# The first two batches of a fused attention and SwiGLU kernel: query copies, scores, the table load and the dummy products in another order

## The chip, the cores and the metric

The kernel runs on one core of a Trainium2 chip. The metric is the device time of one execution in microseconds. Six executions of the kernel before took 236.55 to 238.45 us, median 237.5.

## What is computed

For each of 8 batches and 8 heads, 576 positions of width 64 attend to 32 memory slots; then a SwiGLU block runs over 4608 rows. From the reference:

```
a = softmax(phi)                       # over the 32 slots of each position
k_m = einsum('bhsm,bhsd->bhmd', a, k)  # and v_m from v
attn = softmax(q @ k_m.T / sqrt(64))   # b h s 32
x = (attn @ v_m), rows (b, s), columns (h, d): 4608 x 512
g = x @ w_gate                         # 512 x 1536
out = (silu(g) * (x @ w_val)) @ w_out
```

## The kernel before, in words

Engines: TensorE (PE) multiplies, with PEld its weight loads; VectorE is DVE, ScalarE is ACT, GpSimd is POOL, and SyncE (SP) issues transfers. Each engine takes its instructions in the order in which the program writes them; the whole order is written by hand (`tc.manual_schedule()`), and engines wait for one another through semaphores only.

The work goes by batch. For batches 0 and 1, which are prepared together at the start, each batch passes these steps:

- `phi_exp_masked` (L181): ACT takes exp(phi) into a tile with zeros in the other half of each head pair.
- `k_items` (L337) gives two items. `denominators` multiplies by ones (L244) and takes the reciprocal on DVE (L262, L346). `sums` multiplies keys by exp(phi) in 36 small products (`direct`, L313, products at L319) and copies the result to SBUF in four pieces (L333).
- `q_items` (L822) gives three items, each a call of `q_T` (L371): six transposes of the queries on PE (L377), then one copy of 128x768 from PSUM into `t_qT` by the engine that a letter names, "v" for DVE (L333) or "a" for ACT (L331).
- `scores(b, g)` (L386), for the two head groups g: eight products (L390), then two exponentials on ACT (L401).
- `z_inv(b, g)` (L412): two products with a block matrix of ones (L417), a logarithm of each on ACT (L420), and one exponential of the negative (L422), which is the inverse of the softmax sum.
- `norm(b, g)` (L444): DVE multiplies scores and inverse sums (L446).
- `v_direct` (L361): the same 36 products for the values, and four copies (L333).
- `u_half` (L829) multiplies the values with a half chunk of the gate weights (which = 0) or of the val weights (1), products at L466; the two results leave PSUM by the engines of its letters (ACT L488, DVE L492).
- `gv_gate` (L518) multiplies that with the normed scores (L509), and ACT takes Silu (L526). The val product and the multiplication on DVE (L532) are put in a list and run later by `flush_mul`.

After that the two batches run slot by slot through the weights' three chunks, then the output products (L720) of a batch run beside the next batch.

PSUM is handed out as eight banks in a ring: `bank` takes the first free one, `done` puts it at the end. `warm(n)` (L859) is dummy work: products of the ones matrix with itself, n times 128 columns, at most 512 in one, into a bank that goes back to the head of the ring.

ACT keeps one set of function tables; `preload_act_table_set` (L854, L941) changes it, from exponential and logarithm to Silu and back once for each batch.

The loads of the start come from POOL's queue in the order keys 0, queries 0, keys 1, queries 1, values 0, values 1, then the gate and val weights by halves of the first chunk, then the other chunks (L877 to L908). From the ninth on, POOL waits ahead of an issue for an earlier transfer to land.

The order of the start is this hand-written list (L912 to L951), of which the change touches all but the first lines:

```
    warm(104)
    k0, k1 = k_items(0, "vvvv"), k_items(1, "vvvv")
    q0, q1 = q_items(0, "vvv"), q_items(1, "vvv")
    run(k0)
    warm(8)
    run(k1[:1])
    warm(4)
    run(q0)
```

Of the kernel before, what the change touches and what calls it, by code (L numbers as in the profile page):

```python
# [14 lines left out]
def kernel(  # L15
# [19 lines left out]
    nc = tc.nc  # L35
# [39 lines left out]
    def bank(shape, dtype, name):  # L75
        tag = free.pop(0)
        t = ps.tile(shape, dtype, tag=tag, name=name)
        held[id(t)] = tag, t
        return t

    def done(*tiles):

        for t in tiles:
            free.append(held.pop(id(t))[0])
# [34 lines left out]
    def q_of(b, i, g, r):  # L119

        h = NG * i + g
        return qTs[b][64 * r:64 * r + 64, :, NC * h:NC * h + NC]
# [190 lines left out]
    def direct(b, which):  # L313

        p = bank([128, NP // 2, NG, M], FP32, "p_mT")
        for n in range(NP // 2):
            for j in range(JK):
                for o in range(2):
                    nc.tensor.matmul(  # L319
                        p[64 * o:64 * o + 64, n],  # L320
                        lhsT=kvs[b][:, which, 2 * n + o, j * D:(j + 1) * D],
                        rhs=masked[b][:, j, :, 2 * n + o],
                        start=(j == 0),
                        stop=(j == JK - 1),
                        tile_position=(0, 64 * o),
                    )
        return p

    def copy(eng, out, in_):
        if eng == "a":  # L330
            nc.scalar.copy(out=out, in_=in_)  # L331
        else:
            nc.vector.tensor_copy(out=out, in_=in_)  # L333
# [27 lines left out]
    def v_direct(b, engs):  # L361

        p = direct(b, 1)
        dst = kTs[b][:, 2].rearrange("p (n o m) -> p n o m", n=NP // 2, o=2)
        for x, e in enumerate(engs):
            g, o = x % 2, x // 2
            copy(e, dst[64 * g:64 * g + 64, :, o], p[64 * o:64 * o + 64, :, g])
        done(p)
        scaled.add(b)

    def q_T(b, n, eng="v"):  # L371

        k = NS // 3
        pq = bank([128, k, 128], BF16, "p_q")
        for x in range(k):
            y = k * n + x
            nc.tensor.transpose(pq[:, x], qs[b][:, 128 * y:128 * y + 128], ident)  # L377
        if n == 0:
            qTs[b] = att.tile([128, NS, 128], BF16, tag="qT", name="t_qT")
        copy(eng, qTs[b][:, k * n:k * n + k], pq)  # L380
        done(pq)

    def gv_banks():
        return [bank([128, CH], FP32, f"p_{'gv'[r]}") for r in range(2)]

    def scores(b, g):  # L386
        p = gv_banks()
        for i in range(NP):
            for r in range(2):
                nc.tensor.matmul(  # L390
                    p[r][32 * i:32 * i + 32, 0:HALF],
                    lhsT=kTs[b][64 * r:64 * r + 64, g, 32 * i:32 * i + 32],
                    rhs=q_of(b, i, g, r),
                    start=True,
                    stop=True,
                    tile_position=(64 * r, 32 * i),
                )
        e = att.tile([128, 2, HALF], BF16, tag=f"E{g}", name="t_E")
        for r in range(2):
            scale = rks[b][:, g:g + 1] if b in rks else sm_scale  # L400
            nc.scalar.activation(  # L401
                out=e[:, r].rearrange("p (c s) -> p c s", c=NC),
                in_=p[r][:, 0:HALF].rearrange("p (s c) -> p c s", c=NC),
                func=AF.Exp,
                scale=scale,
            )
        done(*p)
        es[b, g] = e
# [3 lines left out]
    def z_inv(b, g):  # L412

        p = gv_banks()
        lz = att.tile([128, 2, HALF], FP32, tag="lz", bufs=3, name="t_lz")
        for r in range(2):
            nc.tensor.matmul(  # L417
                p[r][:, 0:HALF], lhsT=bones, rhs=es[b, g][:, r], start=True, stop=True
            )
            nc.scalar.activation(out=lz[:, r], in_=p[r][:, 0:HALF], func=AF.Ln)  # L420
        done(*p)
        nc.scalar.activation(out=lz, in_=lz, func=AF.Exp, scale=-1.0)  # L422
        lzs[b, g] = lz
# [20 lines left out]
    def norm(b, g):  # L444
        a = att.tile([128, 2, HALF], BF16, tag=f"A{g}", name="t_A")
        nc.vector.tensor_tensor(out=a, in0=es.pop((b, g)), in1=lzs.pop((b, g)), op=ALU.mult)  # L446
        atts[b, g] = a
# [6 lines left out]
    def u_round(b, parts, evac):  # L454


        banks = []
        for which, c, halves in parts:
            w0, w1, h0, h1 = which[0], which[-1] + 1, halves[0], halves[-1] + 1
            n = (h1 - h0) * HC  # L460
            p = [bank([128, CH], FP32, f"p_u{g}") for g in range(NG)]
            for w in which:
                o = (w - w0) * n
                for i in range(NP):
                    for g in range(NG):
                        nc.tensor.matmul(  # L466
                            p[g][32 * i:32 * i + 32, o:o + n],
                            lhsT=kTs[b][64 * g:64 * g + 64, 2, 32 * i:32 * i + 32],
                            rhs=w_part(w, c, i, g, halves),
                            start=True,  # L470
                            stop=True,
                            tile_position=(64 * g, 32 * i),
                        )
            for g in range(NG):
                if (b, c, g) not in Us:
                    u_buffer(b, c, f"U{c}")
                if len(which) == 1:
                    dst = Us[b, c, g][:, h0:h1, w0]
                else:
                    dst = Us[b, c, g][:, h0]  # L480
                src = p[g][:, 0:(w1 - w0) * n].rearrange("p (a f) -> p a f", f=HC)
                banks.append((dst, src, p[g], rSs[b][:, g:g + 1] if b in scaled else None))
        for (t, p, home, r), e in zip(banks, evac):
            if e == "a":
                if r is None:
                    nc.scalar.copy(out=t, in_=p)  # L486
                else:
                    nc.scalar.activation(out=t, in_=p, func=AF.Copy, scale=r)  # L488
            elif r is None:
                nc.vector.tensor_copy(out=t, in_=p)  # L490
            else:
                nc.vector.tensor_scalar(out=t, in0=p, scalar1=r, scalar2=None, op0=ALU.mult)  # L492
            done(home)
# [328 lines left out]
    def q_items(b, evac):  # L822
        return [lambda n=n: q_T(b, n, evac[n]) for n in range(3)]
# [5 lines left out]
    def u_half(b, which, c, half, evac):  # L829

        return lambda: u_round(b, ((which, c, (half,)),), evac)
# [8 lines left out]
    def run(items):  # L840
        for x in items:
            x()
# [13 lines left out]
    def gv_slots(b):  # L856
        return [lambda s=s: gv_slot(b, s) for s in range(2 * NJF)]

    def warm(n, narrow=0):  # L859


        p = bank([128, DM], FP32, "p_warm")
        x = bones.rearrange("p (a c) -> p a c", a=1)
        sizes = [1] * narrow + [4] * ((n - narrow) // 4)
        sizes += [n - sum(sizes)] if n > sum(sizes) else []
        for a in sizes:
            nc.tensor.matmul(  # L867
                p[:, 0:128 * a],
                lhsT=bones,
                rhs=x.to_broadcast([128, a, 128]) if a > 1 else bones,  # L870
                start=True,
                stop=True,
            )
        free.insert(0, held.pop(id(p))[0])
# [37 lines left out]

    warm(104)
    k0, k1 = k_items(0, "vvvv"), k_items(1, "vvvv")
    q0, q1 = q_items(0, "vvv"), q_items(1, "vvv")
    run(k0)
    warm(8)
    run(k1[:1])
    warm(4)
    run(q0)  # L920
    warm(2)
    scores(0, 0)
    warm(2)
    z_inv(0, 0)
    scores(0, 1)
    warm(6)
    run(k1[1:])
    warm(3)
    z_inv(0, 1)
    run(q1)  # L930
    warm(2)
    scores(1, 0)
    norm(0, 0)
    norm(0, 1)
    warm(3)
    z_inv(1, 0)
    scores(1, 1)
    warm(6)
    v_direct(0, "vvvv")
    z_inv(1, 1)  # L940
    nc.scalar.preload_act_table_set("silu_and_others")  # L941
    norm(1, 0)
    norm(1, 1)
    warm(16)
    v_direct(1, "vvvv")
    warm(4)


    g0, g1 = gv_slots(0), gv_slots(1)
    run([u_half(0, (0,), 0, 0, "av"), u_half(1, (0,), 0, 0, "av")])  # L950
    for s in range(4):  # L951
        gv_gate(0, s)
    run([u_half(0, (1,), 0, 0, "va"), u_half(1, (1,), 0, 0, "va")])
# [158 lines left out]
```

## Time and profile before

| | |
|---|---|
| median of six executions | 237.5 us (236.55 to 238.45) |
| the profiled execution, its own time | 238.29 us |
| its span in the trace | 236.1 us |
| PE busy, share of the span | 226.3 us, 96% |
| DVE, ACT, POOL busy | 183.8, 173.4, 140.7 us |
| mean granted clock of PE | 0.991 |
| dummy products (43 instructions, L867) | 13.4 us of PE busy time |

The span runs from the first to the last instruction of the trace; the execution's own time is 2.19 us longer. Times in views are microseconds from the start of the span. Busy tenths come in 40 slices of 5.9 us; PEclk is the clock that PE was granted, in tenths of full. In a timeline a row says when an instruction or a run of like ones began, how long it took from first start to last end, the engine, the line, what was written from what, and, in brackets, how long the engine had been idle and what ended that. In a table of stretches each engine has its busy time and the number of its instructions, then come the granted clock, the share of the DMA engines and GB/s.

### The profile page before, as it was taken

Reading aid. Unit: us, or ns where it says so; the run is one execution under the profiler, and the core shown is the slowest. Engines: PE = TensorE matmul, PEld = TensorE weight load, DVE = VectorE, ACT = ScalarE, POOL = GpSimd, SP = SyncE. Lnnn points to the kernel's source line nnn. Section 1 sums busy time; section 2 is a strip of 40 time slices with the busy share of each in tenths; the row PEclk is TensorE's granted clock in tenths of the full one; section 3 lists DMA queues with packets and bytes.
Section 4 is the critical chain, followed back from the end, with each engine's and each line's share of the span. In section 5 each row is a group of like instructions: output and inputs, shape, how many; then the busy total and the mean of one; then the engine's idle time right before and its main releaser. Section 6 shows DMA issues by size and latency. Waiting matters only on the chain.

```text
span 236.1 us, 7197 instructions
## 1 busy us (share of the span) xinstructions
PE 226.3 (96%) x2824; PEld 171.5 (73%) x2824; DVE 183.8 (78%) x422; ACT 173.4 (73%) x368; POOL 140.7 (60%) x190
## 2 busy tenths in 40 slices
PE   7977999999999999999999999999999999999992
PEld 2545567678988676887788787887788777878881
DVE  4146679999966798998798767998799879977732
ACT  2745998899456878987896668987898789677220
POOL 8322532999089139854985788554844494039390
PEclk9997999999999999999999999999999999999999
DMA  6999999999993994899099945995022602201224
GB/s 211 210 211 204 200 207 206 245 233 256 204 218 102 227 268 83 194 202 212 4 219 239 226 131 91 251 233 103 3 89 88 126 0 93 87 25 68 58 79 134
DMA packets 36610, 36.84 MB, mean 156 GB/s; under 512 B 14560, under 2 KB 30944, under 8 KB 36576
## 3 DMA queue, kind: packets, MB, share of 16 engines
q0 software_dynamic: 16272, 22.42, 51.2%
q1 hardware_dynamic: 19536, 13.18, 22.0%
q10 hardware_dynamic: 768, 0.79, 1.1%
q8 instruction: 22, 0.36, 0.6%
q14 instruction: 12, 0.10, 0.1%
HBM read 42.47 MB, written 9.44 MB: 220 GB/s over the span
## 4 chain that ended last, share of the span: by engine, by line
PE 93%; DVE 3%; ACT 2%; issue 1%
PE p_g L509 21%; PE p_v L509 20%; PE p_os L720 20%; PE p_oc L720 10%; PE p_oa L720 5%; PE p_u L466 5%; PE p_warm L867 5%; PE p_kv L230 2%; DVE t_qT L333 1%; ACT t_E L401 1%; PE p_mT L319 1%; PE p_g L390 1%; PE p_q L377 1%; DVE t_bkv L266 1%; PE p_S L244 0%
## 5 line engine op out<-in xcount | busy, mean ns | idle before, releaser
L532 DVE TENSOR_TENSOR t_h<-t_sg,p_v 128x288 bf16<-128x288 bf16 x192 | 81.9, 451 | 17.1 <-PE p_v L509 6.9
L509 PEld LDWEIGHTS <-t_U 128*128 128x128 bf16 x768 | 73.6, 98 | 23.1 <-issue 4.0
L526 ACT ACTIVATE t_sg<-p_g 128x288 bf16<-128x288 f32 x192 | 74.1, 423 | 17.8 <-PE p_g L509 11.4
L509 PE MATMUL p_g<-t_A,t_U 128*128 128x288 bf16 x384 | 77.2, 286 | 0.2
L509 PE MATMUL p_v<-t_A,t_U 128*128 128x288 bf16 x384 | 77.2, 286 | 0.0
L720 PEld LDWEIGHTS <-t_S 128*128 128x128 bf16 x384 | 37.5, 98 | 4.5 <-issue 0.2
L597 POOL TENSOR_TENSOR t_S<-t_h 128x512 bf16<-128x512 bf16 x17 | 19.6, 1155 | 34.7 <-DVE t_h L532 34.7
L720 PEld LDWEIGHTS <-t_h 128*128 128x128 bf16 x288 | 27.1, 98 | 8.6 <-issue 5.0
L486 ACT CAST t_U<-p_u 128x512 bf16<-128x512 f32 x53 | 27.9, 606 | 6.6 <-PE p_u L466 6.6
L720 PE MATMUL p_os<-t_T,t_S 128*128 128x256 bf16 x192 | 23.7, 273 | 0.0
L554 POOL TENSOR_TENSOR t_S<-t_S,t_h 128x512 bf16<-128x512 bf16 x17 | 19.7, 1156 | 1.3
L554 POOL TENSOR_TENSOR t_S<-t_h,t_S 128x512 bf16<-128x512 bf16 x16 | 18.4, 1154 | 0.0
L554 POOL TENSOR_TENSOR t_S<-t_h 128x512 bf16<-128x512 bf16 x16 | 18.4, 1153 | 0.0
L466 PE MATMUL p_u<-W,t_kT 64*32 64x512 bf16 (+1 forms) x416 | 16.2, 364 | 0.1
L867 PE MATMUL p_warm<-bones 128*128 128x512 bf16 (+2 forms) x43 | 13.4, 441 | 1.7 <-DVE bones L889 1.7
L720 PE MATMUL p_os<-t_T,t_h 128*128 128x256 bf16 x96 | 14.8, 273 | 0.0
L490 DVE CAST t_U<-p_u 128x512 bf16<-128x512 f32 x19 | 12.4, 682 | 1.9 <-PE p_u L466 1.9
L720 PE MATMUL p_oc<-t_T,t_S 128*128 128x256 bf16 x96 | 12.0, 273 | 0.0
L720 PE MATMUL p_oa<-WO,t_h 128*128 128x256 bf16 x96 | 11.8, 273 | 0.0
L720 PE MATMUL p_oc<-WO,t_S 128*128 128x256 bf16 x96 | 11.8, 272 | 0.0
L720 PE MATMUL p_os<-WO,t_h 128*128 128x256 bf16 x96 | 11.8, 272 | 0.0
L446 DVE TENSOR_TENSOR t_A<-t_E,t_lz 128x576 bf16<-128x576 bf16 x16 | 11.3, 739 | 0.2 <-ACT t_lz L422 0.2
(106 smaller groups left out, 311.3 us busy)
## 6 DMA issues: line engine op xcount, KB each, us to landing
out_dram<-t_o SPq DMA_DIRECT2D x15, 512.0 KB, 3.4
t_kv<-in_k_dram POOLq DMA_DIRECT2D x8, 576.0 KB, 10.2
t_q<-in_q_dram POOLq DMA_DIRECT2D x8, 576.0 KB, 8.7
t_kv<-in_v_dram POOLq DMA_DIRECT2D x8, 576.0 KB, 14.8
t_phi<-in_phi_dram POOLq DMA_DIRECT2D x6, 576.0 KB, 8.3
WO<-in_moe_w_out_dram POOLq DMA_DIRECT2D x3, 512.0 KB, 19.3
W<-in_moe_w_gate_dram POOLq DMA_DIRECT2D x2, 512.0 KB, 16.4
W<-in_moe_w_val_dram POOLq DMA_DIRECT2D x2, 512.0 KB, 15.6
```

The lines of the kernel that those rows point to most:

```text
L230: nc.tensor.matmul(p[g][32 * i:32 * i + 32, 0:n], lhsT=phi_of(b, g, j, i), rhs=kvs[b][64 * g:64 * g + 64, w0:w1, i, j * D:(j + 1) * D], st ...
L446: nc.vector.tensor_tensor(out=a, in0=es.pop((b, g)), in1=lzs.pop((b, g)), op=ALU.mult)
L466: nc.tensor.matmul(p[g][32 * i:32 * i + 32, o:o + n], lhsT=kTs[b][64 * g:64 * g + 64, 2, 32 * i:32 * i + 32], rhs=w_part(w, c, i, g, halve ...
L486: nc.scalar.copy(out=t, in_=p)
L490: nc.vector.tensor_copy(out=t, in_=p)
L509: nc.tensor.matmul(p[:, 0:HALF], lhsT=Us[b, c, g][:, o // 2, which, 128 * (o % 2):128 * (o % 2 + 1)], rhs=atts[b, g][:, r], start=(g == 0) ...
L526: nc.scalar.activation(out=sg, in_=gate[:, 0:HALF], func=AF.Silu)
L532: nc.vector.tensor_tensor(out=dst, in0=sg, in1=val[:, 0:HALF], op=ALU.mult)
L554: eng.tensor_tensor(out=out, in0=x, in1=y, op=ALU.subtract)
L597: eng.tensor_tensor(out=t[:, 0], in0=A21, in1=A22, op=ALU.add)
L720: nc.tensor.matmul(mine[home][:, u], lhsT=lhs(c, m, u), rhs=rhs(c, m), start=fresh and u == 0, stop=(k == 5), skip_group_check=u == 1 or n ...
L867: nc.tensor.matmul(p[:, 0:128 * a], lhsT=bones, rhs=x.to_broadcast([128, a, 128]) if a > 1 else bones, start=True, stop=True,)
```

## The change

Only the hand-written list of the start changes; no function does, and no product that counts is added or removed. The middle one of the three query copies goes to ACT for both batches. The two head groups' scores of a batch stand one after the other. `norm` stands nearer to its inverse sums. `v_direct(0)` stands ahead of `z_inv(1, 0)` in place of behind it. The first gate round of batch 0 stands ahead of the table load, and `norm(1, 1)` after the load; batch 1's first gate round is evicted by DVE twice ("vv" for "av"). The dummies after the first 104 were 8, 4, 2, 2, 6, 3, 2, 3, 6, 16, 4 (56 in all) and are 8, 4, 8, 12, 8, 8, 16, 8 (72), at other places.

```diff
     warm(104)
     k0, k1 = k_items(0, "vvvv"), k_items(1, "vvvv")
-    q0, q1 = q_items(0, "vvv"), q_items(1, "vvv")
+    q0, q1 = q_items(0, "vav"), q_items(1, "vav")
     run(k0)
     warm(8)
     run(k1[:1])
+    run(q0)
     warm(4)
-    run(q0)
-    warm(2)
     scores(0, 0)
-    warm(2)
+    scores(0, 1)
+    warm(8)
     z_inv(0, 0)
-    scores(0, 1)
-    warm(6)
     run(k1[1:])
-    warm(3)
     z_inv(0, 1)
+    norm(0, 0)
+    warm(12)
     run(q1)
-    warm(2)
+    norm(0, 1)
+    warm(8)
     scores(1, 0)
-    norm(0, 0)
-    norm(0, 1)
-    warm(3)
+    scores(1, 1)
+    v_direct(0, "vvvv")
     z_inv(1, 0)
-    scores(1, 1)
-    warm(6)
-    v_direct(0, "vvvv")
+    warm(8)
     z_inv(1, 1)
-    nc.scalar.preload_act_table_set("silu_and_others")
     norm(1, 0)
-    norm(1, 1)
     warm(16)
     v_direct(1, "vvvv")
-    warm(4)
+    warm(8)
 
 
     g0, g1 = gv_slots(0), gv_slots(1)
-    run([u_half(0, (0,), 0, 0, "av"), u_half(1, (0,), 0, 0, "av")])
+    run([u_half(0, (0,), 0, 0, "av")])
+    nc.scalar.preload_act_table_set("silu_and_others")
+    norm(1, 1)
+    run([u_half(1, (0,), 0, 0, "vv")])
     for s in range(4):
         gv_gate(0, s)
```

## The prediction

> **What bounds the kernel now.** I read the two rows of tenths first: where does TensorE (PE) work, and at what clock? Each slice is 5.9 us.
>
> ```profile
> span 236.1 us, 7197 instructions
> ...
> PE   7977999999999999999999999999999999999992
> ...
> PEclk9997999999999999999999999999999999999999
> ```
>
> From the sixth slice (29.5 us) PE is full to the end; before it lie four slices at 7 and one at 9, and in the fourth slice the granted clock sinks to 0.7. In the chain that ended last, the longer pieces after 57 us that are not PE are six, 3.3 us together. So PE is the bound after about 30 us, and what the change edits, all of it between 11.9 and 30 us, is a start-up stage bounded by something else. A microsecond won there is won at the end, if nothing later is waiting for a transfer.
>
> What bounds the start-up? The timelines of ScalarE (ACT), VectorE (DVE) and GpSimd (POOL), 12.5 to 30 us (start, duration, what, and in brackets the idle time before and what ended it; lines 401, 420 and 422 are the exponentials of the scores, the logarithms and the inverse sums, line 333 the query copies, lines 138 and 153 loads of weights, each issued when an earlier transfer, named in its bracket, has landed):
>
> ```profile
> 13.38 1.49 DVE L333 COPY t_qT<-p_q 128x768 bf16<-128x768 bf16 x3 [0.44 <-PE p_q L377]
> 20.41 1.49 DVE L333 COPY t_qT<-p_q 128x768 bf16<-128x768 bf16 x3 [0.58 <-PE p_q L377]
> ```
>
> ```profile
> 15.30 0.50 ACT L401 ACTIVATE t_E<-p_g,t_rk 128x288 bf16<-128x288 f32 x1 [4.71 <-PE p_v L390]
> 19.53 0.41 ACT L420 ACTIVATE t_lz<-p_g 128x288 f32<-128x288 f32 x1 [1.06 <-PE p_g L417]
> 20.27 0.68 ACT L422 ACTIVATE t_lz<-t_lz 128x576 f32<-128x576 f32 x1
> 22.33 0.50 ACT L401 ACTIVATE t_E<-p_g,t_rk 128x288 bf16<-128x288 f32 x1 [1.38 <-PE p_v L390]
> 26.32 0.68 ACT L422 ACTIVATE t_lz<-t_lz 128x576 f32<-128x576 f32 x1
> 27.02 1.28 ACT L941 ACT_TABLE_LOAD   x1
> 28.31 0.47 ACT L488 ACTIVATE t_U<-p_u,t_rS 128x256 bf16<-128x256 f32 x1
> 29.71 1.32 ACT L526 ACTIVATE t_sg<-p_g 128x288 bf16<-128x288 f32 x4
> ```
>
> ```profile
> 18.81 0.74 POOL L138 DMA_DIRECT2D W<-in_moe_w_val_dram  x1 [3.13 <-DMA t_q<-in_q_dram]
> 21.40 0.74 POOL L138 DMA_DIRECT2D W<-in_moe_w_gate_dram  x1 [1.85 <-DMA t_kv<-in_v_dram]
> 24.23 0.74 POOL L138 DMA_DIRECT2D W<-in_moe_w_val_dram  x1 [2.09 <-DMA t_kv<-in_v_dram]
> 25.53 0.74 POOL L153 DMA_DIRECT2D WO<-in_moe_w_out_dram  x1 [0.56 <-DMA W<-in_moe_w_gate_dram]
> ```
>
> It is a relay: transposes, three copies (1.5 us each time), scores, seven ACT pieces per head group, with ACT idle 1.06 and 1.38 us between batches. The POOL rows are a second limit: query 1, values 0 and 1 and the first gate weights are there at about 18.6, 21.15, 24.0 and 25.3 (0.25 ahead of the rows: query 1, issued at 3.97, needs 14.6 us by the view of its tile, so 18.57). Nothing on chip hurries those. The third limit is the clock, by stretches of 3.41 us (PE busy first, PEclk third from the end):
>
> ```profile
> 13.50:16.91 3.41, 2.10 (x31) 1.01 (x28) 1.36 (x3) 1.61 (x4) 0.74 (x1) 1.00 1.10 216
> 16.91:20.33 3.42, 3.31 (x49) 2.35 (x48) 1.16 (x4) 2.30 (x7) 0.74 (x1) 0.50 1.20 204
> 20.33:23.74 3.41, 2.19 (x34) 1.15 (x31) 2.82 (x5) 2.04 (x5) 0.74 (x1) 1.00 1.28 202
> ```
>
> One stretch of 3.42 us runs at half clock. In it the 36 key products take 1.17 us (0.76 at full clock, as at 10.52) and the first six transposes 0.66 (0.51).
>
> **The change, step by step.** Times are those of the profiled execution.
>
> *Queries of batch 0.* warm(4) leaves the place ahead of the transposes, which then follow the denominators (end 12.46) with the gap of 0.14 at worst: 12.55 for 12.84. The group for ACT costs 0.80 there against 0.55 on DVE:
>
> ```profile
> L333 DVE COPY t_qT<-p_q x6: 547/547/556, 13.4 to 21.3; 128x768 bf16<-128x768 bf16 x6
> L331 ACT COPY t_qT<-p_q x3: 799/799/804, 62.4 to 65.0; 128x768 bf16<-128x768 bf16 x3
> ```
>
> Groups are ready at about 13.06, 13.39, 13.73; DVE does the first by 13.65 and the third by 14.3, ACT the second by 14.25. ACT is idle then, so nothing queues behind. Scores start at 14.35 for 14.92: 0.55 won, about 0.3 by the dummy and 0.25 by ACT.
>
> *Both scores in a row.* ACT, from 0.38 after the scores, at a pitch of 0.40: four exponentials 14.7 to 16.3, then two logarithms and the inverse (0.4, 0.43, 0.6), then the same for group 1: its inverse starts at 18.5 and ends at 19.2, for 20.95. That is 0.55 from the start, 1.06 from the idle time at 19.53, and 0.1 of small waits. The key products of batch 1 (landed 14.7) now run at 15.9 to 16.65, before the stretch that was slow. The dummies, warm(8) and (12), are 0.45 and 0.66 at a pitch of 0.22 and end at 15.3 and 17.7, ahead of what follows, so they cost nothing here.
>
> *Queries of batch 1* cannot begin before their landing, 18.57; they began at 19.53. At full clock the groups are ready at 19.15, 19.5 and 19.8; DVE has done norm(0,0) (0.75, from 17.95), ACT its inverse at 19.2, so copies run 19.2, 19.5 and 19.85 to 20.4. Scores (1,0) at 20.45 for 21.95: 1.5 won, nearly 1.0 of it the half clock and the late start, the rest ACT's copy. norm(0,1) stands behind these copies on DVE; nobody wants it before 26.
>
> *Second half of ACT.* Exponentials 20.8 to 22.45, logarithms and inverses to 25.3 (27.0 before; 1.7 won). v_direct(0) now stands ahead of z_inv(1,0) on PE, and waits for its values (21.15) until 21.2, ends at 21.95; the sums behind it are wanted by ACT only at 22.4. Hidden; if the values land 0.5 later it starts to cost.
>
> *The end of start-up.* warm(8), z_inv(1,1) to 23.4, warm(16) (0.9) to 24.3, v_direct(1) (landed 24.0; 0.76) to 25.05, warm(8) to 25.5, then the gate round (weights landed 25.3). About 0.2 of the dummies is on the path: without them the weights would hold the round at 25.3. ACT evicts it at 25.85 (0.47), then loads the table, 26.35 to 27.6, then Silu: 27.65 for 29.71. The table was nearly hidden before (ready 28.30, product ready about 28.2); now Silu's input is ready at 27.0 and waits 0.65 for the table. With the table first, the eviction would end at 27.05 and Silu start at 27.45, so this move costs about 0.2 and brings nothing.
> DVE: four value copies to 26.1, one eviction to 26.6, norm(1,1) to 27.3, then the two "vv" evictions to 28.15. The second value round needs that bank and waits to 28.15 on PE (30.34 before for its neighbour). ACT's four Silu and its copy end at 29.4, and the first val product can go at 29.45 against 31.3 on the chain. So 1.85 to 2.05 is won. The weights' second halves (0.6 MB in 2.8 us at the rate of the POOL rows, so 1.25 us each after 25.3, at 29.3 at the latest) are wanted at 30.3, the next pair (POOL's row for it is at 34.77, so 34.5) at 35.0, query 2 (issued 45.40, 13.7 to landing) at 59.9. All hold, with 0.5 to 1 us left.
>
> **Two rules against it.** On ACT's load: rows 27.02 and 28.31 say 1.29 us to the next operation, and it starts where the inverse ends (27.00). The Trainium skill, "ScalarE: Activation LUTs", What ACT_TABLE_LOAD costs, adds a drain of 1.38, 2.66 in all. By the row Silu starts at 27.65, by the rule at 29.0, and 1.4 of the 2.0 would be gone. I take the row.
> On the clock: "TensorE: Matmul & The Clock Gate", Part 4, says that transposes don't count as busy PE. Of the busy 2.10 and 2.19 above, transposes are 0.51 and 0.75 (the same stretches for their tile). With them, the lower was followed by half clock and the higher wasn't; without them it is 1.59 and 1.44, the wrong way round. So I count them. After the change the stretch 13.5 to 16.9 has about 3.1 busy and the next 2.6 (idle 17.7 to 18.6, waiting for the queries): both above 2.19. By the rule the second is 1.4, and 20.3 to 23.7 would run at half: v_direct(0) and sums +0.35, warm(8) and the rest up to 0.35 more, 0.7 in all.
>
> **The sum.** 2.0 of span: 236.1 to 234.1. The profiled execution took 238.29, 2.19 around its span, so 236.3. It lies 0.8 above the median of the six runs (236.55 to 238.45): the fast ones perhaps had no half clock, and then win only the other 1.0. Between 1.0 and 2.0 off 237.5, I take 1.5: 236.0.
>
> **Rivals.** (A, 0.60) As summed: 235.4 to 236.5.
> (B, 0.18) The half clock only moves, to the scores of batch 1: for it stand 0.9 us of idle PE and the rule; against it the busy shares. 2.0 less 0.7, from 238.29: 237.0; against the median 236.7.
> (C, 0.14) Transfers hold what ACT gives free: landings are read from POOL's wake-ups, and if values 1 and the gate weights come 0.8 later than read, the end of start-up slides with them: 1.2 won at best, and as little as 0.5 in a run without half clock, 237.0. For it: four landings within 0.3 us of their use. Against: each has a row. The table and evictions failing to overlap (the drain) would end there as well.
> (D, 0.08) Slower: the dummies fail to hold the clock and a half-clock stretch falls on 25.5 to 31, where PE has no idle time left. Price up to 3.41/2 = 1.7; with B's 0.7 that is 2.4 against 1.5 won, 238.4, and up to 238.9 where the median run had no half clock. It decides from a busy share under about 2.1 in the stretch that ends near 26; for it only that the stretches may lie elsewhere in another run, against it warm(16) and warm(8).
>
> The range, 235.1 to 237.6, leaves out D and the edge of A. A measurement tells some 0.5% (1.2 us) from no change. Faster by more (under 236.3): 0.8 of A and a tenth or so of B and C, 0.52. Slower by more (over 238.7): 0.06, most of D. The rest, 0.42, within.
>
> **What would show it.** Scores (1,0) near 20.4 and no PEclk under 1 before it; ACT gapless 14.7 to 19.2; transposes of batch 1 starting at 18.6 after a PE wait; table at 26.4, first Silu at 27.65; first val product near 29.4; the rest of the chain equal and 2 us earlier. I am wrong if half clock shows after 20 us, if the gate round waits past 25.5 for weights, or if a later stage (query 2 at 60) waits for a transfer.

## The result, and the profile after

The changed kernel takes 236.44 us (median of 34 executions, 236.05 to 236.82), the kernel before 237.66 (69 executions, 236.51 to 238.69): ratio 0.9947, 95% interval 0.9935 to 0.9958, 1.2 us faster. The forecast was 236.0 in a range of 235.1 to 237.6, so direction and range held. The time is 0.4 us above the forecast; of the gain of 1.5 us that was reckoned from a median of 237.5, 1.2 came. The profiled execution of after took 236.45, 1.85 around its span.

The page of the kernel after: full clock in every slice. The early slices of PE are no fuller (8, 6, 8, 9 for 7, 7, 9 and 9 in the third to sixth): what PE did at half clock counted as busy there, too.

```profile
span 234.6 us, 7201 instructions
...
PE   7986899999999999999999999999999999999992
...
PEclk9999999999999999999999999999999999999999
```

Its ACT timeline shows the relay (copies, scores, exponentials, inverse sums, one waiting for the other) as forecast: one unbroken run from the first exponential (14.18) to the end of the second inverse (17.80 + 0.68), and the second batch done at 25.1 in place of 27.0. Then ACT stands idle for 1.26 us, and the table load comes behind the eviction, the copy of the gate round's result out of PSUM:

```profile
14.18 0.50 ACT L401 ACTIVATE t_E<-p_g,t_rk 128x288 bf16<-128x288 f32 x1 [0.53 <-PE p_v L390]
...
17.80 0.68 ACT L422 ACTIVATE t_lz<-t_lz 128x576 f32<-128x576 f32 x1
...
20.63 0.50 ACT L401 ACTIVATE t_E<-p_g,t_rk 128x288 bf16<-128x288 f32 x1 [0.53 <-PE p_v L390]
...
24.42 0.68 ACT L422 ACTIVATE t_lz<-t_lz 128x576 f32<-128x576 f32 x1
26.37 0.47 ACT L488 ACTIVATE t_U<-p_u,t_rS 128x256 bf16<-128x256 f32 x1 [1.26 <-PE p_u L466]
26.86 1.28 ACT L946 ACT_TABLE_LOAD   x1
28.15 1.32 ACT L526 ACTIVATE t_sg<-p_g 128x288 bf16<-128x288 f32 x4
```

What ACT waits for is PE, and PE waits for transfers, three times in eight microseconds: queries 1, values 0 and the gate weights. In the last two rows it waits for evictions by ACT: for that of the first round itself (26.37 + 0.47), and for one that stands behind four Silu (29.33), and these behind the table load.

```profile
18.42 1.18 PE L377 MATMUL p_q<-ident,t_q 128*128 128x128 bf16 x18 [1.33 <-DMA t_q<-in_q_dram]
...
21.34 0.76 PE L319 MATMUL p_mT<-t_mphi,t_kv 128*64 128x64 bf16 x36 [0.65 <-DMA t_kv<-in_v_dram]
...
26.01 0.41 PE L466 MATMUL p_u<-W,t_kT 64*32 64x256 bf16 x16 [0.43 <-DMA W<-in_moe_w_gate_dram]
26.90 1.15 PE L509 MATMUL p_g<-t_A,t_U 128*128 128x288 bf16 x8 [0.48 <-ACT t_U L488]
...
29.89 0.79 PE L509 MATMUL p_v<-t_A,t_U 128*128 128x288 bf16 x5 [0.38 <-ACT t_U L488]
```

And POOL's timeline, whose rows follow a landing by about 0.25 us: values 1 come 0.17 us later than before, the gate weights 1.76 us behind them where it had been 1.30.

```profile
24.40 0.74 POOL L138 DMA_DIRECT2D W<-in_moe_w_val_dram  x1 [2.08 <-DMA t_kv<-in_v_dram]
26.16 0.74 POOL L153 DMA_DIRECT2D WO<-in_moe_w_out_dram  x1 [1.02 <-DMA W<-in_moe_w_gate_dram]
```

From the round behind the first val products the two chains run alike to the end. In after, then before, it stands at

```profile
30.60 0.63 PE L466 MATMUL p_u<-W,t_kT 64*32 64x256 bf16 x32
```

```profile
32.16 0.63 PE L466 MATMUL p_u<-W,t_kT 64*32 64x256 bf16 x32
```

so the 1.5 us between the spans are all made by then.

**Where the time of before came from.** Each execution's mean granted clock falls into one of two groups. One stretch of 3.42 us at half clock takes 0.007 off the mean of a 236 us span, and the executions of before have either 0.993 and less or 0.997 and more; those of after have 0.995 and more. Grouped so, the executions of before that ran beside the experiments, in four sets, and those of after:

| executions | at half clock for a stretch | median of these | median of the others |
|---|---|---|---|
| before, with e1 to e4 | 14 of 26 | 238.24 | 236.73 |
| before, with g0 to g3 | 18 of 32 | 238.31 | 236.75 |
| before, with h1 to h3 | 13 of 17 | 238.25 | 236.72 |
| before, with k1 | 10 of 13 | 238.45 | 236.82 |
| after | 0 of 34 | | 236.44 |

So the change does two things. In the 55 of 88 executions of before that lose the clock (62%) it wins about 1.8 us, in the others 0.3. 0.62 x 1.8 + 0.38 x 0.3 = 1.2, as much as lies between the medians above; between the means (237.67 and 236.42) it is 1.25. The half-clock executions lie in two clumps themselves, 15 at 237.4 to 237.9 and 40 at 238.1 to 238.8.

### The profile page after: what moved, and what is told of

The parts are those of the page before. It is cut to its first block, busy times and chain, and to the rows that moved or that the text cites. A ratio compares the mean times of both kernels' runs of the same rounds, so it can differ in the third digit from the quotient of the medians.

```text
span 234.6 us, 7201 instructions
## 1 busy us (share of the span) xinstructions
PE 223.8 (95%) x2825; PEld 169.8 (72%) x2825; DVE 183.3 (78%) x421; ACT 173.8 (74%) x369; POOL 140.6 (60%) x190
## 4 chain that ended last, share of the span: by engine, by line
PE 84%; DMA 8%; ACT 2%; POOL 2%; DVE 1%; issue 1%; POOLq 0%
PE p_v L509 20%; PE p_os L720 20%; PE p_g L509 20%; PE p_oc L720 10%; DMA W<-in_moe_w_gate_dram 8%; PE p_oa L720 5%; PE p_u L466 5%; PE p_kv L230 2%; PE p_g L390 1%; POOL t_kv L99 1%; DVE t_bkv L266 1%; POOL t_kv L103 1%; ACT t_sg L526 1%; ACT L946 1%; PE p_q L377 0%
## 5 line engine op out<-in xcount | busy, mean ns | idle before, releaser
L466 PE MATMUL p_u<-W,t_kT 64*32 64x512 bf16 (+1 forms) x416 | 15.6, 363 | 0.5 <-DMA W<-in_moe_w_gate_dram 0.4
L867 PE MATMUL p_warm<-bones 128*128 128x512 bf16 x44 | 13.0, 435 | 1.7 <-DVE bones L889 1.7
```

Of the source, the lines that this page charges most:

```text
L466: nc.tensor.matmul(p[g][32 * i:32 * i + 32, o:o + n], lhsT=kTs[b][64 * g:64 * g + 64, 2, 32 * i:32 * i + 32], rhs=w_part(w, c, i, g, halve ...
L867: nc.tensor.matmul(p[:, 0:128 * a], lhsT=bones, rhs=x.to_broadcast([128, a, 128]) if a > 1 else bones, start=True, stop=True,)
```

## The experiments

Two theories stand against each other; some experiments give them a narrower form. Theory 1: behind the clock, the landing of the first gate weights ends the start-up, and what the relay on chip won beyond it is idle time. Theory 2: the shorter relay (ACT copies, scores in a row, eviction first) is the gain. All kernels are edits of the changed kernel unless it says "before". The executions of before beside each set hold more or fewer with a half-clock stretch, so ratios of different sets aren't comparable among themselves; the medians of the variants are. These repeat to a tenth or so: the changed kernel has 236.44 and, in g0, 236.32.

| run | median us (range) | ratio to before, 95% | with half-clock stretch |
|---|---|---|---|
| e1 table first | 235.80 (235.66 to 236.00) | 0.9947 (0.9925 to 0.9969) | 0 of 7 |
| e2 copies on DVE | 236.12 (235.95 to 236.93) | 0.9963 (0.9946 to 0.9981) | 0 of 12 |
| e3 before, more dummies | 237.08 (236.70 to 237.76) | 0.9985 (0.9963 to 1.0007) | 0 of 12 |
| e4 few dummies | 235.96 (235.74 to 236.39) | 0.9955 (0.9935 to 0.9974) | 4 of 8 |
| g0 after again | 236.32 (235.90 to 236.87) | 0.9942 (0.9919 to 0.9965) | 0 of 12 |
| g1 end undone | 235.87 (235.69 to 236.36) | 0.9936 (0.9911 to 0.9961) | 0 of 9 |
| g2 gate weights earlier | 236.31 (236.01 to 236.55) | 0.9948 (0.9927 to 0.9970) | 0 of 12 |
| g3 gate weights later | 237.71 (237.38 to 238.04) | 1.0012 (0.9992 to 1.0032) | 6 of 12 |
| h1 no load of values 1 | 236.03 (235.69 to 236.31) | 0.9915 (0.9887 to 0.9943) | 0 of 6 |
| h2 before, no load of values 1 | 237.68 (236.70 to 238.89) | 1.0003 (0.9975 to 1.0030) | 10 of 12 |
| h3 table first, copies on DVE | 235.83 (235.63 to 236.25) | 0.9910 (0.9881 to 0.9938) | 0 of 6 |
| k1 program fetch moved | 236.44 (236.24 to 236.65) | 0.9931 (0.9906 to 0.9956) | 0 of 8 |

**e2: the query copies.**

```diff
-    q0, q1 = q_items(0, "vav"), q_items(1, "vav")
+    q0, q1 = q_items(0, "vvv"), q_items(1, "vvv")
```

> The changed kernel with all query copies on VectorE again. Theory 1 (the landing of the first gate weights, 25.87 in the trace of after, sets the end of the start-up, and what was won ahead of it beyond that is idle time): the scores of batch 1 come 0.3 to 0.6 us later, the gate round still starts at about 26.0, time within 0.2 us of the changed kernel, about 236.5. Theory 2 (the shorter ACT and DVE relay is what was won): 0.3 to 0.6 us slower, 236.8 to 237.1.

No slower: 236.12 for 236.44 and 236.32, as theory 1 has it. Its three copies take 1.49 us again, and scores (1, 0) still come at about the same time (first exponential at 20.85 for 20.63). The twelve executions stand in two groups, eight at 235.95 to 236.18 and four at 236.51 to 236.93, without a half clock; the profiled one is of the second, and its gate weights came 2.10 us behind values 1.

**e3: dummies alone, in the kernel before.**

```diff
-    warm(2)
+    warm(8)
     scores(0, 0)
-    warm(2)
+    warm(6)
...
-    warm(2)
+    warm(8)
     scores(1, 0)
...
-    warm(3)
+    warm(6)
     z_inv(1, 0)
```

> The kernel before with four of its dummies enlarged (2, 2, 2, 3 to 8, 6, 8, 6) and nothing else changed. Theory 1: no half-clock stretch, so the slow executions of before (up to 238.7) vanish, and the time is that of the fastest ones, 236.5 to 237.0, ratio about 0.996, most of what the change won. Theory 2: the order and the ACT copies make the gain, so 237.3 or more, no clear change.

Half right. No execution of twelve lost the clock, where 14 of 26 of the unedited kernel beside it did. But the median is 237.08, not 236.5 to 237.0, and 0.35 above the full-clock executions of before: the dummies hold the clock and cost something on the way. What held these twelve apart (236.7 to 237.1, and 237.4 to 237.8) stays open. The interval just holds 1.

**e4: few dummies in the new order.**

```diff
-    warm(4)
+    warm(2)
     scores(0, 0)
     scores(0, 1)
-    warm(8)
+    warm(2)
...
-    warm(12)
+    warm(2)
     run(q1)
     norm(0, 1)
-    warm(8)
+    warm(2)
...
     z_inv(1, 0)
-    warm(8)
+    warm(2)
```

> The changed kernel with its dummies between the queries of batch 0 and the values of batch 1 cut to 2 each (40 less one for one), order unchanged. Theory 1: half-clock stretches come back between 17 and 24 us, but part of what they cost lies in the wait for the gate weights; 236.5 to 237.5, with a wider spread than the changed kernel's 0.8. Theory 2: the clock doesn't matter much here, 236.4 with the same spread.

The half clock is back in four of eight, so it is the dummies that keep it away in the changed kernel. But its price is 0.5 us (medians 236.32 and 235.79), not the 1.5 of before. That what it delays is taken from waits is a guess: the trace is of an execution at full clock. And the median of all eight, 235.96, lies below the changed kernel's 236.44 and 236.32: in this order the added dummies bought a steady clock, but no time. Against before, the order with few dummies wins 1.9 us in the half-clock executions (238.24) and 0.95 in the others (236.73). In the trace the gate weights are there at 25.5 and the round starts at 25.58, where after's first round waits to 26.01. Whether the dummies have a part in when the weights land stays open.

```profile
25.73 0.74 POOL L153 DMA_DIRECT2D WO<-in_moe_w_out_dram  x1 [0.56 <-DMA W<-in_moe_w_gate_dram]
```

```profile
25.58 0.74 PE L466 MATMUL p_u<-W,t_kT 64*32 64x256 bf16 x16
```

The starts of the profiled executions differ too: the second denominators (L244) run at 12.38 here, 11.46 in after. Both have their queries of batch 1 transposed at 18.42 to 18.46, when these land. In these two traces that wait swallows what comes before, which would explain why after's executions lie within 0.8 us.

**e1: the table load back ahead of the round.**

```diff
-    run([u_half(0, (0,), 0, 0, "av")])
     nc.scalar.preload_act_table_set("silu_and_others")
+    run([u_half(0, (0,), 0, 0, "av")])
```

> The changed kernel with the table load put ahead of the first gate round again. In the trace of after ACT is idle from 25.10 to 26.37, waiting for that round, and the load stands from 26.86 to 28.14 behind it. Theory 1: the load (1.28) fits into that idle time, the first Silu comes at about 27.4 for 28.15, the first val products need no second wait, 0.5 to 0.8 us faster, 235.7 to 235.9. Theory 2 (the order of the change is right, eviction first): the eviction is delayed and the time is the same or 0.2 us longer.

0.5 to 0.6 us faster than the changed kernel, and with g1 and h3 the fastest of all, as theory 1 says. ACT's timeline: the load fills the idle time, and the first Silu comes at 27.19 for 28.15, now waiting 0.51 us for PE.

```profile
24.07 0.68 ACT L422 ACTIVATE t_lz<-t_lz 128x576 f32<-128x576 f32 x1
24.77 1.28 ACT L945 ACT_TABLE_LOAD   x1
26.20 0.47 ACT L488 ACTIVATE t_U<-p_u,t_rS 128x256 bf16<-128x256 f32 x1
27.19 1.32 ACT L526 ACTIVATE t_sg<-p_g 128x288 bf16<-128x288 f32 x4 [0.51 <-PE p_g L509]
```

Of the 0.96 us, 0.81 is left at the round of 29.79 (30.60 in after), and 0.79 in the times of the two profiled executions (235.66 and 236.45); the medians are 0.5 to 0.6 apart. A part of it may be the landing, which was 0.17 earlier here (POOL's row at 25.99 for 26.16). The next landing is close: the next round with new weights runs at 34.57 and its weights land at about 34.45 (POOL's row at 34.69).

**g0, the changed kernel again**, for comparison.

> The changed kernel itself, for comparison on the same chip. Both theories: 236.4, no execution with a half-clock stretch (mean granted clock 0.995 or more in all), while about half of those of the kernel before have one (0.990 to 0.992) and take 237.4 to 238.6.

As expected.

**g1: the end as before, but for the last dummies.**

```diff
+    nc.scalar.preload_act_table_set("silu_and_others")
     norm(1, 0)
+    norm(1, 1)
     warm(16)
...
-    run([u_half(0, (0,), 0, 0, "av")])
-    nc.scalar.preload_act_table_set("silu_and_others")
-    norm(1, 1)
-    run([u_half(1, (0,), 0, 0, "vv")])
+    run([u_half(0, (0,), 0, 0, "av"), u_half(1, (0,), 0, 0, "av")])
```

> The changed kernel with the end of its start-up as before: table load and norm(1, 1) ahead of the value products of batch 1, both gate rounds evicted 'av'. Theory 1 (the gate weights' landing sets when the first round starts, about 26.0; what follows it counts): the table load goes into idle ACT time, worth 0.5 to 0.7 as in the run with only that moved, but norm(1, 1) now delays the four value copies and one eviction by up to 0.75; together 235.8 to 236.3. Theory 2 (the new end is part of the gain): 236.6 or more.

0.45 us faster than g0: the change's new end costs about half a microsecond. Theory 2 falls for this part.

**g3: the gate weights one transfer later.**

```diff
     for half in range(2):
-        for which in range(2):
+        for which in ((1, 0) if half == 0 else (0, 1)):
```

> The changed kernel with the first halves of the gate and val weights loaded in the other order, so that the gate half lands one transfer (256 KB, about 1.3 us) later. Theory 1: the first gate round and all behind it slide by it, 0.9 to 1.3 us slower than the changed kernel, 237.3 to 237.7. Theory 2 (the relay on chip is the bound, the landing is hidden): within 0.3 us of it.

1.4 us slower than g0, 1.1 in the executions at full clock. PE's timeline, then ACT's: round and Silu slide by the 1.0 us by which the weights are later.

```profile
26.99 0.41 PE L466 MATMUL p_u<-W,t_kT 64*32 64x256 bf16 x16 [1.31 <-DMA W<-in_moe_w_gate_dram]
```

```profile
29.14 1.02 ACT L526 ACTIVATE t_sg<-p_g 128x288 bf16<-128x288 f32 x3
```

Behind the longer wait there is a half-clock stretch in six of twelve (237.92 for 237.44). In the trace it falls on what follows the wait (PE busy first, PEclk third from the end):

```profile
25.30:28.72 3.42, 1.63 (x25) 0.89 (x24) 2.10 (x7) 1.35 (x2) 1.66 (x3) 1.00 1.42 199
28.72:32.13 3.41, 3.41 (x29) 1.47 (x27) 2.13 (x6) 3.05 (x9) 1.32 (x2) 0.50 1.25 206
```

**g2: the gate weights ahead of values 1.**

```diff
+    load_w(0, 0, 0)
     load_v(1)
-    for half in range(2):
-        for which in range(2):
-            load_w(which, 0, half)
+    load_w(1, 0, 0)
+    for which in range(2):
+        load_w(which, 0, 1)
...
+    nc.scalar.preload_act_table_set("silu_and_others")
+    warm(8)
+    run([u_half(0, (0,), 0, 0, "vv")])
     norm(1, 0)
-    warm(16)
+    for s in range(4):
+        gv_gate(0, s)
     v_direct(1, "vvvv")
+    norm(1, 1)
+    run([u_half(1, (0,), 0, 0, "av")])
```

> The changed kernel with the first half of the gate weights loaded ahead of values 1 (and the val half behind them), the table load ahead of the first gate round, and that round (evicted 'vv') and its four gate products ahead of the value products of batch 1. Theory 1: the gate weights are there 2.8 us earlier, about 23, the round starts right after the sums at 23.5, Silu at about 26.4 when the table is there (28.15 in the changed kernel), values 1 come about 25.5; first val product at about 28.6 to 29.2 for 29.9, 235.1 to 235.8. Theory 2 (ACT's relay bounds): as with the table first alone, 235.8.

A miss: the round ran at 23.65 and Silu at 26.22 as expected, yet the time is that of g0. The wait has only changed its place. Values 1 now come at 25.9, and batch 1's copies and rounds, behind which the val products stand, are as late as ever; PE is at the next weights at 30.29, 0.3 ahead of after:

```profile
26.11 0.74 POOL L153 DMA_DIRECT2D WO<-in_moe_w_out_dram  x1 [2.66 <-DMA t_kv<-in_v_dram]
```

So it seems not to be one transfer that holds the start-up, but all that must have come through the queue by 26 us. This is read from one trace, and g2 moves products as well as transfers.

**h1 and h2: one transfer less, in after and in before.** The load of batch 1's values is left out, and its products read batch 0's.

```diff
-    load_v(1)
...
-                        lhsT=kvs[b][:, which, 2 * n + o, j * D:(j + 1) * D],
+                        lhsT=kvs[b * (1 - which)][:, which, 2 * n + o, j * D:(j + 1) * D],
```

> The changed kernel without the load of batch 1's values: its value products read batch 0's in their place, so that the same products, copies and waits on chip remain and the gate weights land one transfer (576 KB, 2.8 us) earlier, about 23. Theory 1 (the landing of the gate weights is what holds the changed kernel): the first gate round starts when the products and dummies ahead of it allow, about 25.4 for 26.0, Silu at about 27.5 for 28.15, 0.4 to 0.7 us faster, 235.7 to 235.9. Theory 2 (the landing is hidden behind the relay): no difference, 236.3.

> The kernel before with the same load left out in the same way. Theory 1: before, the relay on chip is the bound and the landings are hidden, so nothing changes: 236.7 in executions without a half-clock stretch and about 238.2 in those with one. Theory 2 (both kernels wait alike for transfers): both groups get 0.4 us or more faster.

After gets 0.3 us faster (236.03 for 236.32), less than the expected 0.4 to 0.7; before doesn't (236.76 and 237.94 in its two groups, where the unedited kernel has 236.72 and 238.25; at full clock these are two executions and four). In h1 the weights lie ready at 22.7 and the round starts at 25.68, behind the dummies, 0.33 earlier:

```profile
22.93 0.74 POOL L153 DMA_DIRECT2D WO<-in_moe_w_out_dram  x1 [0.56 <-DMA W<-in_moe_w_gate_dram]
```

```profile
25.68 0.77 PE L466 MATMUL p_u<-W,t_kT 64*32 64x256 bf16 x16
```

So the landing holds the changed kernel by a third of a microsecond, then its dummies hold it, and in before nothing of it shows.

A rival is the four value copies of batch 1 on DVE, which end at 26.06 in after, as late as the round starts; the chain of g0's trace names them. Batch 0's round doesn't read them, and in h1 they run from 25.12 to 26.10 and in e4 from 25.00 to 25.98, and both rounds start ahead of that end.

The trace of h2, an execution of 237.62, adds a second place for the half clock of before's order: 23.05, where the trace of before has 16.91.

```profile
12.81:16.22 3.41, 2.10 (x36) 1.24 (x33) 1.49 (x3) 1.26 (x3) 1.10 (x2) 1.00 1.15 222
19.63:23.05 3.42, 2.11 (x33) 0.91 (x34) 2.18 (x4) 2.25 (x6) 0.91 (x2) 1.00 1.44 196
23.05:26.47 3.42, 3.36 (x50) 1.74 (x45) 2.33 (x6) 3.12 (x7) 2.06 (x3) 0.50 1.37 203
```

Its time is that of the lower clump of before, while 238.29 is in the upper one. That the two clumps are two places of the stretch would fit, but rests on one trace each.

**h3: table first and copies on DVE**, both edits shown above.

> The changed kernel with the table load ahead of the first gate round and all query copies on VectorE: a candidate for the fastest. Theory 1: the 0.3 us that the copies on VectorE cost ahead of scores (1, 0) is lost in the wait for the gate weights, so it runs like the one with the table first alone, 235.7 to 235.9. Theory 2 (the relay counts): 236.0 to 236.3.

The same time as e1: once the table stands first, the ACT copies win nothing that shows. e1 and h3 are faster than both kernels of the study.

**k1: why the weights land later.**

```diff
-    warm(104)
+    warm(104, 8)
```

> The changed kernel with the first two dummy products of 512 columns written as eight of 128: the same dummy columns, six more products and weight loads in TensorE's program. In the traces so far a packet of 16 KB of program (its own DMA queue, 0.95 to 0.97 us) lies at 23.6 to 24.1 us where the gate weights land 1.76 to 2.1 us behind values 1 (five traces), and at 25.0 or later where they land 1.30 behind (three), but two traces with the packet at 24.0 and 24.2 have 1.3 as well. Theory A (the packet keeps one of the 16 DMA engines from its share of the gate weights): twelve more instructions put the packet 1 us or more earlier, the weights land 1.3 behind values 1, near 25.4, and the time is 235.9 to 236.1. Theory B (the packet is a bystander): 1.8 behind still, 236.3 to 236.5.

The suspect is one packet of 16 KB from the queue that the trace calls "instruction". The run settled nothing: the packet moved by only 0.3 us, to 23.5, and the weights came 2.0 behind values 1. Of eleven traces with this order of loads at that point, six of the eight with the packet at 23.5 to 24.2 have a late landing, the other two (g3, h3) have none, and neither have the three with it at 25.0 or after. That the packet is the cause is not shown.

## Why the prediction was right in direction, and 0.4 us off

- **What bounds the kernel:** right. PE's chain from 30 us on took over all that was won ahead of it, and the chain that ended last holds no wait for a transfer from there on. (In the row of tenths, three slices before the sixth are at 7 and two at 9, not four and one; nothing rests on it.)
- **The half clock:** right, and more than half of it all. The prediction took 1.0 of the 2.0 to be the clock and guessed that the fast executions of before had none. The groups show this, at a price of 1.5. e3 and e4 show that the dummies keep it away, with either order.
- **The other 1.0, mis-sized.** An execution of before without the half clock was to win 1.0; it wins 0.3 (236.75 to 236.44). The clock's share was too small and the order's too large, and the forecast lay halfway between the two cases without knowing how often each comes (62 to 38 in 100). That it came within 0.4 us is in part luck. The next points say where the order's share went; with the table load first (e1) it is 0.93 (236.73 to 235.80).
- **Queries and scores:** right. Scores stand 2.34 us behind the second denominators (13.80 less 11.46), 3.05 before: 0.7 won, 0.55 forecast. Transposes of batch 1 at 18.42 (18.57), scores (1, 0) at 20.25 (20.45), last inverse done at 25.1 (25.3). But little of it reaches the end: e2 gives the ACT copies up and loses nothing.
- **The transfers, the step that failed.** The sum had the gate weights "landed 25.3", read from one trace of before, and said that nothing on chip hurries them. That they might be later stood only in rival C, at 0.14, and not in the sum. They landed at 25.9, and the round came at 26.0 for 25.5. That is 0.5 of it in the trace; h1 puts its worth at 0.3.
- **The table load, mis-sized.** It was named as a loss of 0.2, from an eviction due at 25.85. With the round later the idle time ahead of it is 1.26, the whole load fits in, and the loss is 0.5 to 0.6 (e1). The load itself took 1.28 with the next instruction 1.29 behind its start, as the row of before had it. The drain of about 1.38 us that the Trainium skill, "ScalarE: Activation LUTs", What ACT_TABLE_LOAD costs, adds isn't seen.
- **v_direct(0) ahead of z_inv(1, 0):** hidden as forecast. PE waits 0.65 for values 0, and the first logarithm (22.36) follows the last exponential (21.79 + 0.51) by 0.06.
- **The rivals.** B didn't come: no execution of after lost the clock. C (landings later than read) is what happened, by 0.6 at the gate weights and 0.2 at values 1 in place of 0.8. So a sign that the prediction had named for being wrong, the gate round waiting past 25.5 for weights, is there. D's mechanism turned up in g3, at 0.5 us in place of 1.7.
- **What brings the half clock: not found.** The prediction read from two stretches that over 2.1 to 2.19 us of busy PE keep the clock. After's stretch from 16.91 on had 1.88, not 2.6, and kept it, but its stretches may lie elsewhere, as full clock leaves no mark. In a trace with a half-clock stretch they can be laid end to end from that one (an assumption). Then h2's 2.10 from 12.81 and 2.06 in g3 were followed by full clock, before's 2.10 and h2's 2.11 by half clock, so the share alone doesn't decide:

```profile
15.09:18.50 3.41, 2.06 (x43) 1.05 (x41) 1.91 (x5) 3.35 (x9) 0.74 (x1) 1.00 1.09 203
```

  The Trainium skill, "TensorE: Matmul & The Clock Gate", Part 4, says of a transpose that "it doesn't count as PE-busy the same way". Leaving transposes out sorts these stretches worse: 1.59, 1.63 and 2.11 us stand ahead of half clock (before, g3, h2), and 1.24, 1.35 and 1.44 (h2, g3, before) ahead of full clock, beside the 2.06 above, which holds none. So counting them, as the prediction did, fits these traces better, though it isn't enough.

## What to carry to other kernels

When a stage is a relay with loads coming in beside it, list for each load its landing and its use before shortening the relay: what is won beyond the landing that is waited for becomes idle time, and whatever fits in that time (here a table load) belongs there. Look at the clock of each execution, not at one trace: here the spread of the kernel before was one half-clock stretch, on in some executions and off in others. Dummy products can buy steadiness (e3), but compare with the same order without them: in the new order they won no time (e4).

## What the runs showed of the hardware

- The same program had a half-clock stretch in 62% of its executions (55 of 88). In the traces that show one it took 3.41 to 3.42 us and began at 16.91 (before), 23.05 (before's order in h2) and 28.7 (g3). PE's busy share of the stretch ahead doesn't decide it alone.
- Its price isn't fixed: by the medians 1.5 us in before (0.8 and 1.7 in its two clumps), 0.5 in e4 and g3.
- A table load took 1.28 us, and the next operation of ACT started 1.29 us behind its start, in before, after and g2.
- A transfer of 256 KB ended 1.3 us behind the one ahead of it in before, e3, e4 and h3 and 1.8 to 2.1 in after, g0, e1, e2, g1 and k1, with the same queue and order. A packet of 16 KB from the instruction queue holds one DMA engine for about 0.95 us near that point; whether it is the cause or a bystander stays open.
